# Block attention on the two 64x64 corners of each block, and the values' product in two half arrays

## The chip, the cores and the metric

The kernel runs on one core of one Trainium2 chip. The metric is the device time of one execution in microseconds. The kernel before takes 242.04 us in the median of 3 runs (241.68 to 242.35). Matrix products run on TensorE (PE; its weight loads are PEld), elementwise work on VectorE (DVE), ScalarE (ACT) and GpSimd (POOL), and DMAs are issued by SyncE (SP).

## What is computed

The input x has 2048 tokens of 448 features. The result is h2 = h + B(h) with h = x + A(x).

A is attention with 16 heads of 28 features on the normalised x. Token s sees only the eight keys s, s-2, ..., s-14:

```
qkv = layernorm(x) @ wqkv            # 448 -> 3 * 448
idx = pos[:, None] - 2 * arange(8)   # positions below 0 are masked
logits = q . k[idx] * 28 ** -0.5
o = softmax(logits) @ v[idx]
A = o @ wo
```

B is a gated MLP that mixes tokens:

```
z = gelu(layernorm(h) @ w_in)        # 448 -> 2 * 896, halves z1 and z2
g = w_sp @ layernorm(z2) + b_sp      # w_sp is 2048 x 2048, over tokens
B = (z1 * g) @ w_out                 # 896 -> 448
```

## The kernel before

**Who sets the order.** The kernel builds a list of jobs, each with an engine, the operations, what they read and write, and a place in PSUM. `ORDER` (line 26) is a written-out permutation of the jobs, and each engine and the DMA queue of SP work off their jobs in that order, waiting on semaphores where a job needs another's result. `BANK` gives each PSUM ticket its bank, `ON` says which engine does a copy that several could do. PSUM has eight banks of 512 columns; nearly all products take two banks at once, so that about four of them are open at a time.

**Products in halves.** Most products contract over 448 features, in chunks of 64. `product` (line 480) splits each into a part A of eight matmuls and a part B of six, alternately in the upper and the lower 64 rows of the array, into two banks. In part B each bank is served by the other half than in part A, so part B waits until part A has ended, and `apart` demands that another PE job stands between.

**Stages.** x is loaded in six pieces and normalised per 128 tokens (xn). The first four pieces of 128 tokens are transposed by PE, the other twelve by DMA transposes, into xhT. Then the queries and keys (`qk`, five token ranges `QT` by four groups of heads) and V are computed. Attention works on 18 blocks of 112, 114 or (the first) 128 queries; each block sees 128 keys, the queries' own and the 14 or 16 before (`GEOM`, `pad`). After every 256 tokens `project` computes y = o @ wo, h, its norm and the DMA transpose hT. The first and second half of w_in follow (z2, z1; line 825 on), then the product with w_sp (`g`, line 908), the gate, and w_out (line 932). w_in and w_sp are loaded by the same SP queue that issues the transposes.

**The block.** For each block:

- `lg` (line 763), two jobs for heads in two pairs of row strips: one matmul per head, keys stationary (28 rows, 128 columns), the block's queries streamed (112, 114 or 128), each at its own row strip of 32. Heads come in groups of four; head hh of a group lies at rows 32*hh. Each job has two PSUM banks.
- `ex` (line 772), two jobs: ScalarE takes the exponential of all 128 x 8*nq logits into E, bf16.
- `mk` (line 778): VectorE multiplies E by a 0/1 mask `maskb`, the band of the eight keys, the same for all heads.
- `o` (line 787): per head one matmul over all 128 keys, E stationary (128 x 128), V with a column of ones streamed (29 columns), all in one bank.
- `rc`, `om` (lines 795, 798): the reciprocal of the sums, and o times it, into otm; `od` copies the last 64 columns once more, and `oT` is a DMA transpose.

E has four slots, so a block's exp waits for the values' product four blocks before. A small fill (`pads`, line 581) zeroes the columns behind a slot's last head. The matrices of the mask are made by nine steps on GpSimd (line 585 on).

The three kinds of products use the array in different shapes: 64-row halves (`product`), 32-row strips over all columns (`lg`), and the whole array (`o`, `g`, w_out).

## Time and profile before

| what | value |
|---|---|
| runs | 242.04 us median, 241.68 to 242.35 |
| the profiled execution | 240.89 us, of which its span, first to last instruction, 239.2 |
| granted TensorE clock | 1.000 |
| ScalarE: exp, 36 | 32.0 us busy |
| VectorE: mask, 18 | 19.6 us busy |
| PE: logits, 288 matmuls | 92 ns a weight load |
| DMA | 23.26 MB, 66310 packets |

Columns of a group of instructions: line, engine, operation, output<-inputs, shapes, count, then busy time in us and the mean length of one in ns, then the idle time of the engine just before them and what ended it. Matmuls are pipelined: a record of one lasts longer than the time until the next one starts, so what a run of matmuls costs is read from start to start. A timeline row has start, length, engine, line and count, and in brackets the idle time before it.

### The profile page before, as it was taken

The page shows a single profiled execution, that of the slowest core. Times are in us where ns is not written, and L with a number is a line of the kernel's source. Part 1 is how long each engine was busy: PE and PEld are TensorE (multiplying, and loading weights), DVE is VectorE, ACT ScalarE, POOL GpSimd, SP SyncE. Part 2 cuts the span into 40 slices and gives each one's busy share as a digit, 9 for nine tenths or more (in the row PEclk, how much of TensorE's full clock was granted, in tenths as well). Part 3 has the DMA queues.
Part 4 walks back from the last instruction along what each step waited for, and adds up shares of the span by engine and source line. Part 5 has one row for each costly group of instructions (what it writes and reads, how often), then busy time and mean ns, then how long its engine had stood idle before and what let it go on. Part 6 is the DMA issues. An engine that isn't in the chain of part 4 may idle for free.

```text
span 239.2 us, 4969 instructions
## 1 busy us (share of the span) xinstructions
PE 231.4 (97%) x2099; PEld 114.3 (48%) x2110; DVE 152.3 (64%) x323; ACT 92.0 (38%) x113; POOL 35.2 (15%) x73
## 2 busy tenths in 40 slices
PE   7989999799999999999999999999999999999995
PEld 2564464354555644444444444444444444444453
DVE  5799799979989987959877124410751222613674
ACT  3787988768789656687820000000000000000000
POOL 5154220440302030313124000000000000000000
DMA  6943538526668967979999970000000010000032
GB/s 202 340 119 69 137 70 142 89 60 124 148 106 165 171 108 157 154 149 165 168 192 166 186 189 0 3 0 0 0 0 3 31 47 0 0 3 0 26 108 97
DMA packets 66310, 23.26 MB, mean 97 GB/s; under 512 B 58608, under 2 KB 66160, under 8 KB 66288
## 3 DMA queue, kind: packets, MB, share of 16 engines
q1 hardware_dynamic: 66288, 22.95, 47.1%
q8 instruction: 16, 0.26, 0.4%
q14 instruction: 6, 0.05, 0.1%
HBM read 6.83 MB, written 1.84 MB: 36 GB/s over the span
## 4 chain that ended last, share of the span: by engine, by line
PE 81%; DVE 9%; DMA 4%; ACT 2%; SPq 2%; issue 1%; POOL 0%
PE psum L908 40%; PE psum L495 27%; PE psum L932 9%; DMA x_tm<-in_A_x_dram 3%; PE psum L763 2%; PE psum L787 2%; DVE st L607 2%; DVE E L778 2%; DMA xhT<-xn 2%; ACT E L772 1%; DVE z2p L505 1%; DVE otm L798 1%; SPq L520 1%; SPq L519 1%; DVE xn L618 1%
## 5 line engine op out<-in xcount | busy, mean ns | idle before, releaser
L908 PE MATMUL psum<-wsp_hi,z2p 128*128 128x512 bf16 x218 | 50.6, 379 | 0.3
L917 DVE TENSOR_TENSOR ub<-psum,bb 128x512 bf16<-128x512 f32 x28 | 19.2, 689 | 44.4 <-PE psum L908 43.9
L772 ACT ACTIVATE E<-psum 128x896 bf16<-128x896 f32 (+2 forms) x36 | 32.0, 934 | 9.0 <-PE psum L763 9.0
L908 PEld LDWEIGHTS psum<-wsp_hi,z2p 128*128 128x128 bf16 x224 | 21.9, 98 | 26.1
L495 PE MATMUL psum<-xhT,wqk 64*128 64x512 bf16 (+1 forms) x280 | 27.1, 334 | 2.0 <-DMA xhT<-xn 1.6
L908 PE MATMUL psum<-wsp_lb,z2p 128*128 128x512 bf16 x108 | 26.1, 379 | 0.2
L908 PE MATMUL psum<-wsp_la,z2p 128*128 128x512 bf16 x111 | 25.9, 379 | 0.2 <-issue 0.2
L495 PE MATMUL psum<-w_in,hnT 64*128 64x448 bf16 x224 | 24.8, 349 | 0.1
L495 PE MATMUL psum<-hnT,w_in 64*128 64x512 bf16 x196 | 24.1, 376 | 0.0
L939 DVE TENSOR_TENSOR srg<-psum,x_tm 128x448 bf16<-128x448 f32 (+1 forms) x17 | 9.7, 592 | 20.8 <-PE psum L932 20.7
L932 PE MATMUL psum<-w_out,z1p 128*128 128x448 bf16 (+1 forms) x119 | 22.3, 341 | 0.0
L843 DVE BATCH_NORM_STATS2 st<-z2p 128x6 f32<-128x448 bf16 x32 | 18.9, 609 | 3.7 <-ACT z2p L836 3.4
L778 DVE TENSOR_TENSOR E<-E,maskb 128x1792 bf16<-128x1792 bf16 (+2 forms) x18 | 19.6, 1095 | 1.7 <-ACT E L772 1.6
L607 DVE BATCH_NORM_STATS2 st<-x_tm 128x6 f32<-128x448 bf16 x32 | 19.4, 612 | 1.6 <-DMA x_tm<-in_A_x_dram 1.4
L602 POOL TENSOR_TENSOR rs<-rs,negh 128x2 f32<-128x2 f32 (+2 forms) x22 | 18.9, 857 | 1.8
L495 PEld LDWEIGHTS psum<-xhT,wqk 64*128 64x128 bf16 x280 | 12.8, 94 | 12.3 <-ACT E L772 2.4
L908 PEld LDWEIGHTS psum<-wsp_la,z2p 128*128 128x128 bf16 x112 | 10.9, 98 | 13.4 <-DVE z2p L852 0.4
L908 PEld LDWEIGHTS psum<-wsp_lb,z2p 128*128 128x128 bf16 x112 | 11.0, 98 | 13.2
L932 PEld LDWEIGHTS psum<-w_out,z1p 128*128 128x128 bf16 x119 | 11.6, 98 | 10.2 <-DVE z1p L920 0.3
L880 ACT ACTIVATE z1p<-psum 128x1024 bf16<-128x1024 f32 x14 | 14.2, 1023 | 5.2 <-PE psum L495 5.1
L495 PEld LDWEIGHTS psum<-w_in,hnT 64*128 64x128 bf16 x224 | 10.6, 94 | 11.0 <-DVE z2p L505 0.6
L601 POOL TENSOR_SCALAR rs<-mv 128x2 f32<-128x2 f32 (+2 forms) x22 | 6.3, 288 | 62.1 <-DVE mv L609 41.3
(54 smaller groups left out, 226.2 us busy)
## 6 DMA issues: line engine op xcount, KB each, us to landing
w_in<-in_B_w_in_dram SPq DMA_DIRECT2D x8, 224.0 KB, 3.0
out_dram<-srg SPq DMA_DIRECT2D x16, 112.0 KB, 1.7
x_tm<-in_A_x_dram SPq DMA_DIRECT2D x3, 448.0 KB, 6.1
wraw<-in_A_wqkv_dram SPq DMA_DIRECT2D x2, 448.0 KB, 4.1
w_out<-in_B_w_out_dram SPq DMA_DIRECT2D x1, 784.0 KB, 6.4
bb<-in_B_b_sp_dram SPq DMA_DIRECT2D x1, 512.0 KB, 5.8
wv<-in_A_wqkv_dram SPq DMA_DIRECT2D x2, 224.0 KB, 6.3
wo<-in_A_wo_dram SPq DMA_DIRECT2D x1, 336.0 KB, 7.7
```

What stands on the lines that cost most here:

```text
L495: ins = e.matmul(out(k), w(k, p0, c), x(k, p0, c), start=(k, p0, c) in first, stop=(k, p0, c) in last, tile_position=(p0, 0))
L601: [(lambda e: e.tensor_single_scalar(A, mv[:, m:m + n, 1], EPS, ALU.add), r_mv[k][m:m + n], [rr]), (lambda e: e.tensor_tensor(R, A, negh[: ...
L602: (lambda e: e.tensor_tensor(R, A, negh[:, 0:1].to_broadcast([128, n]), ALU.pow), [rr, r_negh], r_rs[k][m:m + n])],
L607: [(lambda e: e.bn_stats(st[:, m, :], src), [rsrc], [r_st[k][m]])], dve_t(D))
L772: return e.activation(o, i, AF.Exp, scale=SCALE)
L778: return e.tensor_tensor(a, a, maskb[:, 0:1, pad:pad + nq].to_broadcast([NK, NHEAD, nq]), ALU.mult)
L843: [(lambda e, m=m, k=k: e.bn_stats(st3[:, m, k, :], z2p[:, m, D * k:D * (k + 1)]), [r_z2[m]], [r_st[2][m]])], dve_t(D))
L880: return e.activation(o, i, AF.Gelu_apprx_tanh)
L908: ins = e.matmul(psv(tk), z2p[:, s, 128 * fc:128 * fc + 128], w[:, 512 * (tc % 2):512 * (tc % 2) + 512], start=(s == 0), stop=(s == NB - 1))
L917: [(lambda e, tc=tc, s=s, tk=tk: e.tensor_tensor(ub[:, s, :], psv(tk), bb[:, 512 * tc:512 * tc + 512], ALU.add), [r_bb], [r_ub[s]])], dve_ ...
L932: ins = e.matmul(psv(tk, 0, c1 - c0), z1p[:, fc, 128 * m:128 * m + 128], w_out[:, fc, c0:c1], start=(fc == 0), stop=(fc == FC7 - 1))
L939: [(lambda e, m=m, s=s, tk=tk, c0=c0, c1=c1: e.tensor_tensor(srg[:, s, c0:c1], psv(tk, 0, c1 - c0), x_tm[:, m, c0:c1], ALU.add), [r_x[m]], ...
```

## The change

**Logits.** A block's 128 keys are cut at 64. Keys 0 to 63 are seen only by the block's first 64 queries (78 in block 0) and keys 64 to 127 only by its last 64. So each head has two matmuls of 64 keys by 64 queries, at column tiles 0 and 64 of its row strip: the upper one writes PSUM partitions 0 to 63, the lower one 64 to 127. From block 1 on all 16 heads share one ticket of two banks, 64 columns per head; the second job `lg_1` writes the same banks from other strips and must wait for the end of `lg_0`.

**Exp and mask.** From block 1 on one exp of 1024 columns per block, and a mask of 16 x 64 columns, at a stride of 128 in E. The other 64 columns of each head stay zero; they are filled once at the start per slot (`pads0` to `pads3`, two on VectorE and two on GpSimd), and `padsx` clears 14 columns after block 0. The mask is made in 14 steps instead of nine, with three variants.

**Values' product.** Per head two matmuls with 64 keys each, one per 64-row half of the array, with the same 128 x 128 reading of E (zeros beside the corner); heads 0 to 7 and 8 to 15 have a bank each, and, as in `product`, part B serves each bank from the other half. The ticket has two banks, and `rc` and `om` read both.

**Order.** `ORDER`, `BANK` and `ON` are new for all jobs. On PE logits now stand mostly in groups of four halves (`lg4_0 lg5_0 lg4_1 lg5_1`), once of eight, in eight stretches; parts A and B of the values' product stand between parts of other products. On VectorE the fills `pads2` and `pads0` come before the first statistics and between the first two normalisations; normalisations 2 and 3 come before the statistics of rows 4 to 7 are all done. On SP some w_in loads and the transposes of w_sp for slices 6, 1, 4 and 7 come earlier, among the transposes of xn and o.

```
-        pool("pads", -58, [(lambda e: e.memset(E[:, :, NHEAD * 112:NHEAD * 114 + 14], 0.0), ...
+        def ez(i):
+            return E[:, i, 0:NHEAD * 128].rearrange("p (h c) -> p h c", c=128)[:, :, 0:64]
+        for i in range(NE):
+            move_z("pads%d" % i, [(lambda e, i=i: e.memset(ez(i), 0.0), [], [r_Ez[i]]),
...
+            wd, u0 = (78, 64) if b == 0 else (64, nq - 64)
+            tk2 = Ticket(2)
             for j in range(2):
-                tk = Ticket(2)
+                tk = Ticket(2) if b == 0 else tk2
...
-                            c = (tk.b + i) * 512 + 128 * g
-                            ins = e.matmul(psum[:, c:c + nq], qkT[p:p + DH, 2 * g + 1, k0:k0 + NK],
-                                           qkT[p:p + DH, 2 * g, t0:t0 + nq], start=True, stop=True,
-                                           tile_position=(p, 0))
+                            c = (tk.b + i) * 512 + (128 * g if b == 0 else 64 * (4 * j + g))
+                            for r in range(2):
+                                ins = e.matmul(psum[64 * r:64 * r + 64, c:c + wd], qkT[p:p + DH, 2 * g + 1, k0 + 64 * r:k0 + 64 * r + 64],
+                                               qkT[p:p + DH, 2 * g, t0 + u0 * r:t0 + u0 * r + wd], start=True, stop=True,
+                                               tile_position=(p, 64 * r))
...
+                if b and not j:
+                    continue
...
+            if b:
+                pl.apart.append((lgs[(b, 0)], lgs[(b, 1)]))
...
-                        ins = e.matmul(psum[:, tk.b * 512 + 32 * h:tk.b * 512 + 32 * h + DH + 1],
-                                       E[:, slot, ei * nq:ei * nq + 128], V1[:, vs, h, 0:DH + 1],
-                                       start=True, stop=True)
+                        for r in range(2):
+                            k = part ^ r
+                            ei = 8 * (hh % 2) + 4 * (hh // 2) + 2 * k + gg
+                            c = (tk.b + k) * 512 + 32 * (4 * gg + hh)
+                            a = 64 + 128 * ei - u0 * r
+                            ins = e.matmul(psum[:, c:c + DH + 1], E[64 * r:64 * r + 64, slot, a:a + 128],
+                                           V1[64 * r:64 * r + 64, vs, 4 * (2 * k + gg) + hh, 0:DH + 1], start=part + gg + hh == 0, stop=part + gg + hh == 5,
+                                           tile_position=(64 * r, 0))
```

## The prediction

> **What bounds the kernel now.** The page first: busy time by engine, two rows of the forty slices, and the shares of the chain that ended last.

> ```profile
> span 239.2 us, 4969 instructions
> ...
> PE 231.4 (97%) x2099; PEld 114.3 (48%) x2110; DVE 152.3 (64%) x323; ACT 92.0 (38%) x113; POOL 35.2 (15%) x73
> ...
> PE   7989999799999999999999999999999999999995
> ...
> DVE  5799799979989987959877124410751222613674
> ...
> PE 81%; DVE 9%; DMA 4%; ACT 2%; SPq 2%; issue 1%; POOL 0%
> ```

> TensorE is busy nearly throughout, and the chain that ended last lies on it for 81%. A busy PE may still run under its rate, so the next views are the waits, and the stretch from the start of the query and key product of tokens 512 on to the first product with w_sp (start and end, length, then busy time of PE, PEld, DVE, ACT, POOL).

> ```profile
> POOL rs L601 <- DVE mv L609: 41.3, 12, 7.8
> ...
> PE psum L495 <- DMA xhT<-xn: 1.6, 1, 1.6
> ...
> PE psum L647 <- DVE xn L618: 0.8, 1, 0.8
> ```
> ```profile
> 21.20:118.70 97.50, 95.61 (x1323) 48.62 (x1321) 85.77 (x178) 75.17 (x87) 21.94 (x38) 1.00 0.72 130
> ```

> In the waits (us in total, times, longest) PE waits visibly for two things, 2.4 us together, at full granted clock (1.00). In the window, which ends at that first product, VectorE is busy 85.8 and ScalarE 75.2 of 97.5 us, and PE 95.6. So work taken from ScalarE and VectorE is worth only the waits that it ends. What else the change can bring must come from PE's own time for logits and values' product. From the first product with w_sp on the change computes nothing differently; only the order of products differs, PE has no gap there now, and I take the rest as a constant.

> The price of these products is start to start, since records of matmuls overlap. In the chain of waits, and in the timeline of PE below it, they read:

> ```profile
> 23.42 4.42 PE psum L495 x40
> 27.84 0.90 PE psum L787 x32
> 28.74 0.30 PE psum L763 x8
> ...
> 30.42 0.49 PE psum L787 x16
> ...
> 32.43 0.33 PE psum L763 x16
> ...
> 118.70 10.74 PE psum L908 x49
> ```
> ```profile
> 51.23 0.92 PE L495 MATMUL psum<-wv,xhT 64*128 64x448 bf16 x8
> 51.98 0.81 PE L495 MATMUL psum<-xhT,wqk 64*128 64x512 bf16 x6
> ...
> 58.42 0.92 PE L495 MATMUL psum<-wv,xhT 64*128 64x448 bf16 x8
> 59.27 0.96 PE L787 MATMUL psum<-V,E 128*128 128x29 bf16 x32
> ...
> 78.21 1.76 PE L787 MATMUL psum<-V,E 128*128 128x29 bf16 x64
> 79.91 0.93 PE L495 MATMUL psum<-w_in,hnT 64*128 64x448 bf16 x8
> ```

> Sixteen value matmuls take 0.49, 64 take 79.91 - 78.21 = 1.70: (1.70 - 0.49)/48 = 25 ns each, and 0.09, say 0.10, once per run. Eight half-array matmuls take 51.98 - 51.23 = 0.75 before another half-array product, but 59.27 - 58.42 = 0.85 before the values' product: entering another shape of the array costs 0.10, leaving it 0.10 again (that second one is inside the 0.49 and 0.33). Eight logits matmuls on two row strips, four per strip, take 0.30: 0.10 for leaving, and 50 ns from one to the next on a strip. Sixteen on four strips take 0.33: the strips run side by side. Forty matmuls of the query and key product take 4.42, 0.22 a pair.

> **Part by part: the values' product.** Before: 288 x 25 ns + 11 runs x 0.10 = 8.3 us.

> ```profile
> L787 PE MATMUL psum<-V,E 128*128 128x29 bf16 x288 | 9.0, 176 | 0.0
> ...
> L763 PEld LDWEIGHTS psum<-qkT 28*128 28x128 bf16 x288 | 5.0, 92 | 5.5 <-issue 1.6 <-ACT E L772 1.1 <-DVE xn L618 0.7
> ...
> L763 PE MATMUL psum<-qkT 28*128 28x112 bf16 x144 | 4.7, 210 | 0.0
> ```
> ```profile
> 13.40 0.37 PE L763 MATMUL psum<-qkT 28*128 28x112 bf16 x8
> ...
> 71.72 0.40 PE L763 MATMUL psum<-qkT 28*128 28x114 bf16 x16
> ```

> After: 576 matmuls on 64 rows, alternately in the two halves, in 36 jobs of 16. If the halves run side by side, a job is 8 x 25 ns = 0.20 and all are 7.2 us; if not, it is 16 x 25 ns = 0.40 and all are 14.4. Less than 25 ns on one piece of the array no row shows. I take 7.2, as sixteen logits matmuls in 0.33 already beat 16 x 25 = 0.40. The array's shape is now that of the products around it, so no switch: -1.1 us. The part-B job waits for part A's end; one other job lies between always, so I cost that at nothing; uncovered it would be about 0.2 (a matmul's 176 ns) each.

> Entries into other shapes: before, the nineteen logits runs (the first and the last are above) and eleven value runs form 23 stretches, 2.3 us; after, eight logits stretches, 0.8. That is -1.5.

> **Logits.** Before: 17 runs x 0.33 + 2 x 0.30 = 6.2 us. After: 36 halves of 16 matmuls, four on each of four tiles (two row strips by two column halves), 64 columns streamed instead of 112, 64 columns of weights instead of 128. No row shows a column tile. Lower bound: 25 ns per interval, the shortest of any row, 0.10 a half. Upper bound: the load is not hidden at all, 92 ns from its row and 50 x 64/112 = 28 ns of streaming, 120 ns, 0.48 a half. I take 50 ns, 0.20 a half, the nearest row (the run of eight: same strips, loads hidden, though twice as many columns loaded and streamed). In a group of four halves, first halves a0 and b0 of two blocks, then a1 and b1 into the same banks: a1 starts when a0's last result is in, 0.15 + 0.21 = 0.36; b1 ends at 0.20 + 0.36 + 0.20 = 0.76; leaving makes 0.86 for two blocks, 7.7 us for eighteen. By the same steps 25 ns gives 0.59 and 5.3 us, 120 ns gives 1.75 and 15.7. So +1.5, between -0.9 and +9.5.

> [...]

> **Exp, mask, fills.**

> ```profile
> L772 ACT ACTIVATE E<-psum 128x896 bf16<-128x896 f32 x18 | 16.1, 923 | 5.3 <-PE psum L763 5.3
> ...
> L778 DVE TENSOR_TENSOR E<-E,maskb 128x1792 bf16<-128x1792 bf16 x9 | 9.8, 1086 | 1.7 <-ACT E L772 1.6
> ...
> L772 ACT ACTIVATE E<-psum 128x1024 bf16<-128x1024 f32 x2 | 2.0, 1024 | 0.6 <-PE psum L763 0.5
> ...
> L778 DVE TENSOR_TENSOR E<-E,maskb 128x2048 bf16<-128x2048 bf16 x1 | 1.2, 1215 | 0.0
> ```
> ```profile
> 1.51 0.48 DVE L582 MEMSET otm<- 128x512 uint32 x1
> ...
> 5.55 0.41 DVE L618 TENSOR_SCALAR xn<-x_tm,mv,rs 128x512 bf16<-128x512 bf16 x1 [0.47 <-POOL rs L602]
> ```

> Seventeen blocks have one exp of 1024 instead of two of about 900: 2 x 0.92 - 1.02 = 0.82 each, 14 us off ScalarE. The mask falls from 1792 to 1024 columns at (1215 - 1086)/256 = 0.5 ns: 1.09 to 0.70, 6.6 us off VectorE; if the strided form lost its rate the saving would be nothing. The fills cost VectorE twice 0.5 (the 1024 values go in pairs, like the 0.48 above) to 1.0 at the start, and one of about 0.3 after block 0's product, with block 0's scaling (om0) queued behind it. One start fill stands between the first two normalisations, with 0.47 us of idle time as cover; it may push the second by 0.1 to 0.5, and I cost that at nothing because ScalarE's weight repack stands before the copy that needs it. Two fills and five more mask steps go to GpSimd, which idles for 41 us in all before statistics (its wait for DVE mv). Copies that change engine go about as many each way; I take them as nothing. All this is off the path; its worth is the waits.

> **Waits.**

> ```profile
> 7.65 3.32 PE L495 MATMUL psum<-xhT,wqk 64*128 64x256 bf16 x56 [0.34 <-ACT xhT L505]
> ...
> 12.74 0.72 PE L647 MATMUL psum<-ident,xn 128*128 128x128 bf16 x8 [0.80 <-DVE xn L618]
> ...
> 47.41 1.04 PE L495 MATMUL psum<-xhT,wqk 64*128 64x512 bf16 x8 [1.62 <-DMA xhT<-xn]
> ```
> ```profile
> 14.39 12.73 SPq L519 DMA_TRANSPOSE xhT<-xn  x8
> ...
> 36.05 1.20 SPq L519 DMA_TRANSPOSE xhT<-xn  x1
> ...
> 40.56 4.97 SPq L519 DMA_TRANSPOSE xhT<-xn  x3
> ```

> The 0.80 falls because normalisations 2 and 3 no longer stand behind the statistics of rows 4 to 7 on VectorE. Half is given back: two w_in loads go ahead of the first transposes, and row 4's normalisation comes some 0.6 after the old 14.39, at about 1.3 us a transpose, so the product for tokens 512 on, which starts at 21.2 now, starts near 21.4; meanwhile PE does later blocks' work. Net -0.5 (0 to -0.8). The 1.62 falls because the last four normalisations stand around mask 5 on VectorE. From 21.4 PE does 28 pairs for tokens 512 on (6.1), seven more (1.5), blocks 0 to 2's values (1.2) and the logits of 4 and 5 (1.0): 31; exp and mask make 33, the four with what stands between 37. On SP two w_in loads, wlo1, oT3 and oT4 stand among these transposes; seven or eight issues of 1.3 or less start the last by about 43, and like the others it lands 2 to 3 us on, at 46. It is needed after the whole of the two products for tokens 512 and 1024 on (12.2), V for three pairs of blocks (4.0 at 0.19 a pair), two output projections (2.7), values of blocks 0 to 6 (2.8) and logits of 4 to 11 (3.8): 47, or 48 with small waits. That is -1.6; if the cover of 1 to 2 us is gone, it stays. New: pairs of blocks take their PSUM banks together, four blocks all eight, so PE meets an exp or a V copy still running; about four places x 0.2, +0.8 (0 to 2).

> **Sum.** -1.1 - 1.5 + 1.5 - 0.5 - 1.6 + 0.8 = -2.4 us. The profiled execution took 240.89, its span 239.2 and 1.7 around it; its forecast is 238.5. The median of the runs is 242.04, 1.15 above that execution, so the forecast on its scale is 239.6.

> **Rivals.** (1) Cheaper logits: tiles at 25 ns. -2.4 - 2.4 = -4.8, 237.2. For it: fewer columns loaded and streamed than in the row I took. (2) No change: the products gain 1.1, but transposes or PSUM banks make PE wait as before, or the product gain is used up. 0 to -0.5, about 242. For it: VectorE's many 9s up to slice 20, and SP's queue. (3) Slower: loads of column tiles show. At 120 ns the logits take 15.7 instead of 7.7: +8.0 - 2.4 = +5.6, 247.6. It decides from about 77 ns per interval, where two blocks cost 1.29 instead of 0.86 and the 2.4 is gone. Against it: loads hide on row strips now, as 50 ns with a 92 ns load shows. [...] (4) It does not do what it says: the array's halves take turns in the values' product, +7.2 - 2.4 = +4.8, 246.8. Against it: 0.33 for sixteen.

> **Numbers.** Forecast 0.47, its own range 238.1 to 241.1; (1) 0.15, (2) 0.16, (3) 0.16, (4) 0.06. About 0.3% (0.7 us) is what a measurement can tell from no change. Faster: nearly all of the forecast and (1), 0.61; same 0.15; slower 0.24, from (3), (4) and a bad (2). The range goes from 236.8, (1) with fewer new waits, to 244.5, which takes in (2) and (3) to about 90 ns, and leaves out the rest of (3) and (4).

> **What would show it.** Right: value matmuls at 8 x 25 ns per 16 with no gap to their neighbours; a group of four logits halves near 0.86; no PE wait on xhT near 47; the product with w_sp starting near 116.3 instead of 118.7; about 120.5 after it, as now. Wrong: that start after 118; intervals above 77 ns on a column tile; PE rows that wait on ACT E or on V copies for over 2 us in all; a later first product than 7.65.

## The result and the profile after

The changed kernel takes 246.64 us in the median of four executions (244.38 to 248.66), beside 242.19 for the kernel before. The ratio of the two is taken over their faster executions alone, here 245.12 and 244.38, since 248.17 and 248.66 lie over 1.5% above the fastest: 1.011 times as long (95% interval 1.007 to 1.015). Measured again it was 1.017 (1.009 to 1.025) and 1.011 (1.006 to 1.016). It is slower; the forecast was 1% faster. The profiled execution took 245.12, 4.23 more than the one before.

The page of the changed kernel: the first line counts all instructions, PEclk is the granted clock of TensorE in tenths by slices of a fortieth, q8 is the DMA queue that the page calls `instruction` (packets, MB, share); its packets have 16,384 bytes each.

```profile
span 243.4 us, 6131 instructions
...
PEclk9999997999999999999999999999999999999999
...
q8 instruction: 21, 0.34, 0.6%
```

And the same queue in the kernel before:

```profile
q8 instruction: 16, 0.26, 0.4%
```

There are 1162 instructions more, five more packets, and one slice with a lower clock. I take the packets for TensorE's instructions: its records (products, weight loads, its sequencer's) are 4268 before and 5433 after, 267 and 259 to a packet. The waits of TensorE in the changed kernel (who waited <- for whom: us in all, times, longest):

```profile
PE psum L496 <- DMA OT<-otm: 1.8, 1, 1.8
...
PE psum L665 <- DVE xn L636: 0.9, 2, 0.7
PE psum L496 <- DMA xhT<-xn: 0.7, 1, 0.7
PE psum L496 <- DVE OT L506: 0.6, 1, 0.6
PE psum L785 <- DVE qkT L506: 0.6, 1, 0.6
PE psum L820 <- DVE E L807: 0.6, 1, 0.6
PE psum L973 <- DVE z1p L961: 0.4, 1, 0.4
PE psum L820 <- issue: 0.2, 1, 0.2
```

The wait of 1.62 us for xhT near 47 us is gone, as forecast. In its place stand one of 1.8 us for a transposed attention output and a row of waits of about half a microsecond. (A name in front of a line number is what is written: `qkT` the queries and keys, E the exponentials, OT the transposed output, xhT the transposed input.) The chain of the same execution (start, length, what):

```profile
33.80 4.36 DMA OT<-otm
38.30 2.50 PE psum L496 x14
...
122.17 51.91 PE psum L949 x240
```

The transpose of block 2's output (oT2) is issued at 33.80 and lands at 38.16. The w_sp product starts at 122.17; it was 118.70 before, and 116.3 by forecast. What follows the long wait shows in a table by stretches (columns after the length: busy time and count for PE, PEld, DVE, ACT, POOL; then the granted clock):

```profile
37.50:38.30 0.80, 0.01 (x1) 0.04 (x2) 0.00 (x0) 0.80 (x2) 0.00 (x0) 1.00 0.33 33
38.30:40.00 1.70, 1.70 (x12) 0.88 (x14) 0.00 (x0) 0.20 (x1) 0.00 (x0) 0.64 0.70 190
40.00:41.50 1.50, 1.50 (x24) 0.77 (x22) 0.00 (x0) 0.65 (x1) 0.00 (x0) 0.50 0.76 128
41.50:43.00 1.50, 1.50 (x27) 0.91 (x24) 0.82 (x1) 0.37 (x1) 0.00 (x0) 0.77 0.90 165
```

From 38.79 on, by the trace's clock records, the clock is at one half for 3.41 us, which costs TensorE 1.7 us.

The products themselves, in the timeline of TensorE (start, length, line, count):

```profile
31.86 0.87 PE L785 MATMUL psum<-qkT 28*64 28x64 bf16 x64
32.66 1.04 PE L496 MATMUL psum<-xhT,wqk 64*128 64x512 bf16 x8
```

Four logits halves take 0.80 from start to start (0.86 by forecast). And at the start, VectorE's timeline:

```profile
4.68 0.41 DVE L636 TENSOR_SCALAR xn<-x_tm,mv,rs 128x512 bf16<-128x512 bf16 x1 [0.29 <-POOL rs L620]
5.15 0.48 DVE L592 MEMSET E<- 128x512 uint32 x1
5.70 0.09 DVE L593 MEMSET E<- 128x32 uint32 x1
5.71 0.87 DVE L636 TENSOR_SCALAR xn<-x_tm,mv,rs 128x512 bf16<-128x512 bf16 x1
```

The fill stands between the first two normalisations, and the second takes 0.87 where it took 0.41: GpSimd fills another slot of E at that time. The first product of TensorE starts at 8.04 instead of 7.65.

Where the 4.2 us are, from start to start in both traces:

| part | forecast | measured |
|---|---|---|
| first product | 0 | +0.4 |
| products: values, shapes, logits | -1.1 | -0.2 by the rows after and the prediction's count of before, -0.9 by the rows of both (the shapes' -1.5 taken as forecast); -0.5 by what is left over |
| waits over 0.15 us ahead of the w_sp product | -1.3 | +2.0 (2.4 in two places, now 4.4 in six) |
| halved clock | none | +1.7 |
| behind the start of the w_sp product | 0 | +0.6 |

(The chain gives +0.7 for the last, 120.5 to 121.2; the trace of before lacks the record of the first w_sp product, 0.2 us, so that its row of 118.70 is late by that. The wait for z1p lengthens one interval by 0.59.)

### The profile page after: what moved, and what is told of

Its sections match the earlier page's. It is cut to its first block, busy times and chain, and to the rows that moved or that the text cites. A ratio compares the mean times of both kernels' runs of the same rounds, so it can differ in the third digit from the quotient of the medians.

```text
span 243.4 us, 6131 instructions
## 1 busy us (share of the span) xinstructions
PE 233.3 (96%) x2688; PEld 120.4 (49%) x2688; DVE 146.5 (60%) x327; ACT 81.8 (34%) x99; POOL 33.4 (14%) x79
## 3 DMA queue, kind: packets, MB, share of 16 engines
HBM read 6.83 MB, written 1.84 MB: 36 GB/s over the span
## 4 chain that ended last, share of the span: by engine, by line
PE 78%; DVE 9%; DMA 7%; ACT 2%; issue 1%; POOL 1%; SPq 1%; POOLq 0%
PE psum L949 38%; PE psum L496 28%; PE psum L973 8%; DVE st L625 2%; DMA x_tm<-in_A_x_dram 2%; PE psum L820 2%; DMA OT<-otm 2%; DMA OTs<-otm 2%; DMA xhT<-xn 2%; DVE E L807 1%; DVE xn L636 1%; DVE ub L958 1%; ACT qkT L506 1%; DVE mv L627 1%; POOL rs L620 1%
## 5 line engine op out<-in xcount | busy, mean ns | idle before, releaser
L496 PE MATMUL psum<-xhT,wqk 64*128 64x512 bf16 (+1 forms) x280 | 29.1, 339 | 0.7 <-DMA xhT<-xn 0.7
L506 ACT ACTIVATE qkT<-psum 128x1024 bf16<-128x1024 f32 (+1 forms) x18 | 15.3, 859 | 16.1 <-PE psum L496 16.1
L798 ACT ACTIVATE E<-psum 128x1024 bf16<-128x1024 f32 x17 | 16.6, 1028 | 4.0 <-PE psum L785 3.8
L620 POOL TENSOR_TENSOR rs<-rs,negh 128x2 f32<-128x2 f32 (+2 forms) x22 | 17.1, 776 | 1.8
L496 PE MATMUL psum<-wo,OT 64*128 64x448 bf16 x112 | 14.2, 367 | 2.5 <-DMA OT<-otm 1.8
L820 PEld LDWEIGHTS psum<-V,E 64*128 64x128 bf16 x576 | 12.3, 93 | 8.6 <-DVE E L807 1.9
L496 PEld LDWEIGHTS psum<-w_in,hnT 64*128 64x128 bf16 x224 | 11.3, 94 | 9.6 <-ACT OT L506 0.2
```

Source lines behind the costliest of these rows:

```text
L496: ins = e.matmul(out(k), w(k, p0, c), x(k, p0, c), start=(k, p0, c) in first, stop=(k, p0, c) in last, tile_position=(p0, 0))
L506: j = pl.job(name, eng, key, [(lambda e: e.activation(o(), i(), AF.Copy) if eng == "act" else e.tensor_copy(o(), i()), list(reads), list(w ...
L620: (lambda e: e.tensor_tensor(R, A, negh[:, 0:1].to_broadcast([128, n]), ALU.pow), [rr, r_negh], r_rs[k][m:m + n])],
L798: return e.activation(o[:, :, :, 0:64], psum[:, tk.b * 512:tk.b * 512 + 1024].rearrange("p (i h q) -> p i h q", i=2, q=64), AF.Exp, scale= ...
L820: ins = e.matmul(psum[:, c:c + DH + 1], E[64 * r:64 * r + 64, slot, a:a + 128], V1[64 * r:64 * r + 64, vs, 4 * (2 * k + gg) + hh, 0:DH + 1 ...
```

## The experiments

The theory after the traces: the products came out near the forecast, and the time was lost in the new order, through a late transpose and the clock after it, VectorE beside GpSimd's fills, and the tail. The first rival: the new products cost more than their rows show. The second: what makes transposes late, instruction fetches, is there in any order.

### 1. The changed kernel again, and four edits of its order

**e0_control**, no edit.

> The changed kernel again, unaltered, on the chip and in the job of the three runs beside it, as their yardstick. Theory (the time was lost in waits, not in the products): 244 to 246 us; TensorE waits about 1.8 us near 36.4 us of the span for the transposed output oT2, its granted clock then stands at 0.5 for about 3.4 us, the w_sp product starts near 122.2 us and about 121.2 us follow it. Rival (the 245 us of the first profile was one unlucky execution): within 0.3% of the kernel before, and the wait near 36.4 us not there or short.

245.85 us median of four, 1.017 (1.009 to 1.025). The profiled execution took 243.65, and there the wait for oT2 and the halved clock are both absent. So neither is a constant of this kernel. Its oT2 stands at the same place in the queue and is issued at 33.26, and it lands 2.46 us later instead of 4.36; the queue's order alone doesn't make the long wait. Still this execution is 2.7 us longer than the one before: first product +0.4, waits +2.2 (eight of 0.2 to 0.8), tail +0.6, products -0.5. Of 18 executions of the changed program 11 have a clock below 1, seven of them by two such spells (0.985 or 0.986); of 115 executions of the kernel before 62 have one, all of them by a single spell (0.992 or 0.993). The halved clock is in both kernels; two spells in one execution are in the changed one alone.

**e1_sp_order**: jobs on SyncE's queue.

```
-xTdma8 w_in1_1 wlo6 oT1 oT0 oT2 xTdma14 w_in1_0 oT3 wlo1 xTdma13
+xTdma8 oT1 w_in1_1 oT0 oT2 xTdma14 oT3 xTdma13 w_in0_0 ... xTdma15 w_in1_0 ... hT8 wlo6 hT10 wlo1
```

> The changed kernel with four weight loads later in SyncE's written order (second half of w_in1 behind the transpose oT1, the w_lo load 6 behind hT8, w_lo load 1 behind hT10, first half of w_in1 behind the last xT transpose), so that the transposes oT0 and oT2 are issued some 2 to 4 us earlier; nothing that TensorE computes is altered. Theory (the new order put these loads ahead of oT2 on SyncE's queue, TensorE waits 1.8 us for it and its clock is then halved for 3.4 us, which costs another 1.7 us): wait and clock dip near 37 us go, the w_sp product starts 2.5 to 3.6 us earlier, near 119, and the time falls to 241.5 to 243 us. Rival 1 (the column-tiled logits and the halved values' product cost TensorE itself more): the wait goes but the time stays within 0.7 us, since the products and not the wait are what came on. Rival 2 (the transposes are late because instruction fetches fall on their DMA engines, wherever they stand in the order): another transpose is late by 1 to 2 us instead, and the time falls by less than 1 us.

243.52 us, 1.005 (1.002 to 1.009): faster than the changed kernel, by about half of what was expected. In its chain:

```profile
120.95 51.91 PE psum L940 x240
```

The w_sp product starts 1.2 us earlier than at first, not 2.5 to 3.6, and 0.3 later than in e0_control, whose transpose had landed in time without help. In this profile the long wait is gone, and the short ones stand as before. Four of its ten executions still have a lower clock, three of them by two spells.

**e2_fills**: VectorE and GpSimd (fill 0 to 3 are `pads0` to `pads3`).

```
-DVE: n0_0 pads0 n0_1 wp0_1_0        POOL: rs0_1 pads1 ... mask13 pads3
+DVE: n0_0 n0_1 pads0 wp0_1_0 ... st0_10 pads1      POOL: mask12 pads3 mask13
```

> The changed kernel with the start's zero fills of E moved: fill 0 on VectorE behind the second normalisation instead of between the first and the second, fill 1 from GpSimd to VectorE behind the statistics of block 10, fill 3 on GpSimd behind the last mask operation. Theory (VectorE is held up by the fill itself, 0.57 us, and runs at half speed while GpSimd fills): the second normalisation takes 0.4 us again instead of 0.86, the normalisation of block 8 0.4 to 0.6 instead of 1.17, TensorE's first product starts near 7.65 instead of 8.04 us, block 1's mask is done earlier, and the time falls by 0.4 to 1 us, as far as nothing behind it (the wait for oT2 near 36.4 us) takes it back; the waits later in the span keep their places. Rival (the start's delay is absorbed by the wait near 36 us): the first product comes earlier by 0.4 us, and the time stays within 0.2 us.

245.66 us, 1.013 (1.005 to 1.021): no gain. VectorE's timeline shows that the mechanism is there:

```profile
5.64 0.41 DVE L627 TENSOR_SCALAR xn<-x_tm,mv,rs 128x512 bf16<-128x512 bf16 x1 [0.47 <-POOL rs L611]
6.11 0.48 DVE L583 MEMSET E<- 128x512 uint32 x1
```

The second normalisation is back at 0.41, that of block 8 went from 1.17 to 0.40, and the wait for block 1's mask is gone. But the fill now stands ahead of the weight copies, the first product starts at 8.54, and in the profiled execution a transpose later on (oT4) was late by 3.2 us, with a halved clock behind it. The theory was right on the operations and wrong on the time.

**e3_hold_clock**: a job ahead of the output projection of block 0.

```
+pl.job("hold", "pe", 1e6, [(lambda e: [e.matmul(psv(tkh, 0, 128), ident[:], ident[:], start=True, stop=True)
+                                       for _ in range(27)][-1], [r_ident], [])], 1.5, acq=tkh)
```

> The changed kernel with 27 products of the identity matrix (128 columns, about 1.5 us at full clock, into a free PSUM bank that nobody reads) on TensorE in the idle time just ahead of the output projection of block 0, where it waits 1.8 us for oT2. They compute nothing that the output uses. Theory (TensorE's idle time of 1.8 us is what makes the granted clock stand at 0.5 for the next 3.4 us): the wait itself stays, since oT2 lands no earlier, but the clock stays near 1.0 from 38 to 42 us and the time falls by about 1.7 us, to near 243.4. Rival (the dip's cause is something else, the load of the column-tiled products just ahead, or a throttle that comes at times of its own): the clock falls to 0.5 all the same, and the time rises by up to 1.5 us or stays.

The stretches around it in TensorE's clock:

```profile
36.00:37.50 1.50, 1.50 (x78) 1.43 (x77) 1.50 (x4) 0.68 (x2) 0.63 (x1) 1.00 0.42 79
37.50:40.00 2.50, 2.50 (x43) 1.67 (x42) 0.27 (x1) 1.42 (x2) 0.00 (x0) 1.00 0.55 134
40.00:42.00 2.00, 2.00 (x52) 1.20 (x48) 1.14 (x2) 1.02 (x1) 0.00 (x0) 1.00 0.60 122
```

oT2 lands at 38.10 here too, and the clock stays at 1.00: at this place the idle time halves it, and without the idle time the products ahead of it don't. Three of four executions had a clock of 0.999 or more. That part holds. The time doesn't follow: 247.19 us, 1.020 (1.014 to 1.025), against an expected 243.4. TensorE stops elsewhere, for 1.2 us near 64 in the middle of a run of logits that wait for nothing, and 0.5 near 49; it also waits 1.6 for a transpose hT near 109 and 1.1 near 23.6. The stops were the first sign of what section 6 settles.

**e4_both**, e1_sp_order and e2_fills together.

> The later weight loads of e1_sp_order and the moved fills of e2_fills together, everything else as in the changed kernel. Theory (two separate losses of the new order, and the waits for the mask of block 1 and for the second normalisation go with the fills): the fills give 0.4 to 0.9 us beside the 1.1 to 2.2 us of the later loads, so 242 to 243 us, level with the kernel before or up to 0.4% slower; no wait of over 1.5 us ahead of the w_sp product and no halved clock in most executions. Rival (a wait that is taken away is given back at the next late transfer): the time stays within 0.2% of e1_sp_order.

245.60 us, 1.014 (1.007 to 1.021), worse than e1_sp_order alone. No wait exceeds 0.9 us, yet every execution has a halved clock; in the profile three waits of 0.25 to 0.85 us stand within five microseconds ahead of it. Neither the theory nor the rival expected a loss.

### 2. More instructions, and the old order

**e5_nops** and **e6_phase** were to add empty instructions, to the kernel before and to the changed one.

```
+for _ in range(3):
+    e.nop()
 ins = e.matmul(out(k), w(k, p0, c), x(k, p0, c), ...
...
-block.tensor(lambda eng: sch.emit("pe", eng))
+block.tensor(lambda eng: ([eng.nop() for _ in range(128)], sch.emit("pe", eng)))
```

> The kernel before with 1113 empty instructions (NoOp) on TensorE, three ahead of each product of the stages qk, v, y and z2; nothing is computed otherwise. They bring TensorE's instructions to 5,320, near the changed kernel's 5,376. Theory (instructions are fetched in blocks of 16 KB over the same DMA engines; each fetch lengthens a DMA-transpose issue by 0.7 to 1.2 us and makes transposes land late): the instruction queue's packets rise from 16 to 20 or 21, more of SyncE's transpose issues ahead of 90 us take 1.8 us or longer, TensorE waits longer for transposes, and the time rises by 0.5 to 2.5 us, with the product intervals unchanged. Rival 1 (fetches are hidden): the packets rise and the time stays within 0.3%. Rival 2 (empty instructions cost TensorE itself): the intervals of the products with the added instructions grow, evenly.

> The changed kernel with 128 empty instructions (8 KB, half of a fetched block) ahead of TensorE's first work, where TensorE waits for data anyway; all else as it was. Theory (a late transpose is one on which an instruction fetch falls): every fetch comes half a block earlier, some 2 to 2.5 us in the stretch from 25 to 85 us; the issue of transpose oT0, which took 1.86 to 2.64 us in all five traces of the changed kernel's orders, takes 1.3 us, another transpose some 2 us ahead of it in the order takes about 2, and which waits show changes with it. The time changes by up to 2 us in either direction. Rival (oT0 is slow for what stands ahead of it in the queue): the same issues stay long, the waits keep their places.

The programs hold no empty instructions: 16 and 21 packets, as without them. So the two runs are repeats: 0.9998 (0.995 to 1.004) for the kernel before, 1.011 (1.006 to 1.016) for the changed one. They say nothing on fetches.

**e7_old_order**: `ORDER` and `ON` of before on the changed jobs, PSUM banks handed out first-free.

> The changed kernel's products, exp, mask and fills (fills where e2_fills has them) in the order of the kernel before: its order of jobs, its engines for the copies, and PSUM banks handed out first-free; the second half of a block's logits and of its values' product stands one TensorE job behind the first half. Theory (the products by themselves are worth about nothing and the new order lost the time): 240.5 to 242.5 us, within 0.3% of the kernel before or faster, and the w_sp product starts near 118.5 us. Rival (the new products, with two PSUM banks for the logits of 16 heads and two for the values' product, make TensorE wait for banks whatever the order): TensorE waits for ACT's exp and DVE's normalisation by more than 3 us in all, and the time is 244 us or more.

267.08 us, 1.101 (1.093 to 1.110). TensorE waits 13 us in 22 places ahead of the w_sp product, and its clock is halved for 20.5 us in three spells of 6.83. The longest row of waits:

```profile
PE psum L487 <- DVE otm L831: 4.0, 6, 1.1
```

These are PSUM banks that block results hold until VectorE has scaled them. The run fits the rival, but my bank choice is part of it, so it doesn't separate products from order. One thing it shows: with the old order of the tail, from the first w_sp product to the last product it is 118.06 us, against 118.67 in the changed order.

### 3. Position in the program, the tail, one corner

**e9_phase**: five of the first warming products replaced.

```
+pl.job("phase", "pe", 1e6, [(lambda e: [e.matmul(psv(tkp, 0, 8), warm[:, 0:128], warm[:, 0:8], start=True, stop=True)
+                                        for _ in range(64)][-1], [r_warm], [])], 1.5, acq=tkp)
```

> The changed kernel, with five of the warming products at TensorE's start replaced by 64 narrow ones (8 columns), which brings 118 more instructions, nearly half of a fetched block of 256, ahead of all that follows; TensorE waits for data there anyway. Theory (TensorE runs out of instructions: in every trace of the changed order it stops 0.2 to 1.2 us in the middle of a run of products that wait for nothing, behind the eight logits halves of blocks 12 to 15, and goes on some 2.5 us after an instruction packet set out): every packet comes about half a block earlier in the program, so the stop near 64 to 66 us moves to another place in that dense stretch or goes, the issue of transpose oT0, 1.9 to 2.6 us in most traces so far, falls back to about 1.3 and another transpose ahead of it takes about 2. The time changes by up to 1.5 us in either direction. Rival (the stops hang on the data, not on the fetches): the stop stays in the same value product, and the same issues stay long.

247.36 us, 1.019 (1.013 to 1.026). The stop in mid-product is gone from 64 us and from all the stages (0.24 us stand ahead of a warming product at 4.0), but the issue of oT0 takes 1.75 us, not the 1.3 that was expected. But the start is lost:

```profile
7.09 2.34 PE L979 MATMUL psum<-warm 128*128 128x512 bf16 x5
9.36 0.34 PE L487 MATMUL psum<-xhT,wqk 64*128 64x256 bf16 x2
```

Five warming products take 2.3 us where they took 1.2 in e0_control, 427 ns from start to start instead of 216, so TensorE ran at half the rate. The first product starts 1.3 us later, which spoils the time as evidence. That the stop went speaks for the theory.

**e10_tail**: TensorE and VectorE.

```
-PE: g3_3_3 wo11_0 g2_3_1 wo9_0 wo4_0 ... g5_3_3 wo8_0 wo12_0
+PE: g3_3_3 wo11_0 g2_3_1 wo9_0 ... g5_3_3 wo4_0 wo8_0 wo12_0
```

> The changed kernel with the output product of token block 4 moved behind the last group of the w_sp product, so that two output products instead of one stand between that group and the product which needs its last result. Theory (the tail of the new order is 0.6 us longer than the old one for that single wait of TensorE for VectorE's z1p): the wait goes, and from the first w_sp product to the last product of TensorE it is 118.1 us instead of 118.7; the time falls by 0.5 to 0.6 us against the changed kernel, whatever the earlier waits do. Rival (VectorE's last steps are the bound, not their place): the wait moves to the next output product and the tail stays at 118.5 us or more.

245.17 us, 1.010 (1.005 to 1.014). The wait for z1p is gone, and the tail is 118.06 us, as in the old order (117.84 in its trace, which lacks the record of the first w_sp product, 0.22). The 0.6 us are there; the long wait and the clock ahead of it come as before (1.8 us in its profile).

**e11_tuned**: e1_sp_order, e10_tail, the loads w_in2_0 and w_in3_0 behind hT0, fill 0 behind the weight copies, fill 1 on VectorE and fill 3 early, qe1_0 (a copy of queries and keys out of PSUM) ahead of the statistics of block 11.

> The changed kernel with the later weight loads of e1_sp_order, two more of them behind the transpose hT0 (so that oT8, whose landing frees the buffer that block 11's result waits for, is issued 1.3 us sooner), the tail of e10_tail, the zero fills of E moved out of the first normalisations' way and behind the weights' copies, and the copy qe1_0 one statistics step earlier on VectorE. Theory (the loss is waits of the new order, each of which can be moved out of the way): first TensorE product near 7.8 us instead of 8.05, no wait for qe1_0 and for block 1's mask near 18 to 22 us, none for om11 near 60, tail 118.1; in all 2 to 3 us below the changed kernel, 241.5 to 243 us, within 0.4% of the kernel before on either side. Rival (what is won ahead is waited for at the next late transpose or instruction packet): no more than 1.5 us below the changed kernel, above 243.5.

243.71 us, 1.007 (1.003 to 1.010): 2 us below the changed kernel and 0.7 above the theory's 243, with two new waits of 0.6 us at the start where the fills went and one of 1.2 for a mask near 23.

**e12_onetile**:

```
-for r in range(2):
-    ins = e.matmul(psum[64 * r:64 * r + 64, c:c + wd], qkT[p:p + DH, 2 * g + 1, k0 + 64 * r:k0 + 64 * r + 64], ...
+ins = e.matmul(psum[:, c:c + wd], qkT[p:p + DH, 2 * g + 1, k0:k0 + NK],
+               qkT[p:p + DH, 2 * g, t0:t0 + wd], start=True, stop=True, tile_position=(p, 0))
```

> The changed kernel with one logits product per head over all 128 keys and the block's first 64 or 78 queries, in place of two of 64 keys: the second corner is left out (its place holds logits of other queries), and 288 products and as many weight loads go; exp, mask, values' product and order stay. Theory (column-tiled logits cost TensorE some 1.5 us themselves, and their instructions come faster than they are fetched): instruction packets fall from 21 to 18 or 19, the stop in the middle of a values' product near 64 us goes, the logits' busy time falls by 1.5 to 3.5 us, idle time ahead of the w_sp product by 0.5 to 1; 240 to 243 us. Rival 1 (loads of the tiles were hidden and the instructions too): the time stays within 0.5% of the changed kernel, since the waits of the order take up what the logits give. Rival 2 (the stop is a wait for data): it stays.

244.43 us, 1.007 (1.002 to 1.011). In its page and timeline:

```profile
q8 instruction: 19, 0.31, 0.6%
```
```profile
31.90 0.76 PE L775 MATMUL psum<-qkT 28*128 28x64 bf16 x32
32.59 1.04 PE L487 MATMUL psum<-xhT,wqk 64*128 64x512 bf16 x8
```

Half the products take 0.69 from start to start instead of 0.80. The column tiles cost 0.1 us a group, 1.0 us of the logits' busy time in all (8.1 in e0_control, 7.0 here), less than the 1.5 to 3.5 expected; the time is above the 240 to 243 expected. Packets fall to 19 and the stop goes, as the theory had it; the idle time falls by 0.4 only, since a wait of 1.0 us for a PSUM bank takes its place. With the rows of the values' product in the changed kernel (8.1 us against 8.3) the first rival of this chapter, dear products, falls.

### 4. The same work in more instructions

**e13_split**, on the kernel before.

```
+cut = 2 if name[0] in "qvy" and n > 256 else 1
...
+    for s in range(cut):
...
+            ins = e.matmul(o[:, s * h:s * h + h], w(k, p0, c), v[:, s * h:s * h + h], ...
```

> The kernel before, in its own order, with each wide product of the stages qk, v and y (512 or 448 columns) issued as two of half the width: the same sums, 406 more products and as many more weight loads, 812 instructions or some 3 packets of 256, all ahead of 75 us. Theory (instruction packets lengthen transpose issues and make them land late): packets ahead of 90 us rise from 10 to 13, SyncE's transpose issues of over 1.5 us from 5 or 6 to 8 or more, nearly all of them over a packet; TensorE's idle time ahead of the w_sp product rises by 0.5 to 2 us with its busy time within 0.5 us, and the time by 0.3 to 1%. Rival 1 (fetches are hidden, and the new order alone makes late transposes matter): as many more packets and long issues, but idle time and time the same within 0.3%. Rival 2 (half-width products show their weight loads): the busy time rises by more than 1 us.

244.69 us, 1.012 (1.007 to 1.016). In its stretches (PE's busy time is the second number):

```profile
8.26:121.04 112.78, 109.35 (x1928) 76.85 (x1930) 98.23 (x213) 85.94 (x104) 26.07 (x51) 1.00 0.75 132
121.04:240.30 119.26, 117.50 (x556) 55.14 (x565) 49.41 (x100) 2.63 (x3) 4.21 (x8) 1.00 0.23 51
```

Busy time rises by 1.1 us (rival 2: half-width products show their loads), idle time ahead of the w_sp product by 0.7, the first product starts 0.6 later, and one wait of 1.2 us near the end is a matter of result buffers. Packets ahead of 90 us are 12, long transpose issues 6, hardly more than in the kernel before. So this run doesn't show that packets alone make a kernel slower; whether late transposes cost time in an order not packed so densely stays open.

### 5. Taking the waits away

**e14_best**: e1_sp_order, e10_tail, w_in2_0 and w_in3_0 behind hT0. **e15_best2**: also fill 3 behind mask step 12. **e16_best3**: also

```
-DVE: n0_2 n0_3 st0_7         POOL: od13     PE: y10A o16A y10B z2_6A o16B
+DVE: st0_7 n0_2 n0_3  od13                  PE: o16A y10A o16B y10B z2_6A
```

> The changed kernel with the later weight loads of e1_sp_order, two more behind the transpose hT0, and the tail of e10_tail; the fills stay as changed. Theory (three separate losses of the new order): 1.1 to 2.2 us from the loads, 0.6 from the tail, up to 0.4 from oT8: 242 to 243 us, within 0.3% of the kernel before, and most executions without a halved clock. Rival (with 14 instruction packets ahead of 90 us some transpose is late in any order): still 0.4% or more slower than the kernel before, with a halved clock in every second execution.

> As e14_best, with fill 3 of E earlier on GpSimd (behind the mask step 12), so that the normalisation of block 8 doesn't run beside it. Theory (VectorE is held up while GpSimd fills, and block 1's mask with it): the normalisation of block 8 takes 0.4 instead of 1.17 us, the wait of 0.56 us for block 1's mask near 21.7 us goes, and the time is 0.2 to 0.5 us below e14_best. Rival (the next transpose, xT of block 7, lands no earlier and takes the gain back): no difference beyond 0.2 us.

> As e15_best2, with the statistics of block 7 ahead of the normalisation of block 2 on VectorE (in 0.65 us that stood idle there, so that blocks 4 to 7 are normalised and their transposes issued 0.6 us sooner), od13 on VectorE instead of GpSimd (0.18 instead of 0.63 us, so that transpose oT13 is issued sooner), and block 16's values' product ahead of the output projection that waits for oT13. Theory (the gain of the products, some 0.5 us, is behind the waits): the waits near 22 and 77.5 us shrink from 0.8 and 0.7 us to 0.3 or less each, and the time falls by 0.5 to 1.2 us against e15_best2, to 241.3 to 242, 0 to 0.4% below the kernel before. Rival (each wait taken away comes back at the next late transpose or instruction packet): within 0.2% of e15_best2.

e14_best: 242.70 us, 1.003 (1.000 to 1.007); six of its twelve executions have a halved clock, as its rival had it. e15_best2: 242.47, 1.002 (0.999 to 1.005); the normalisation of block 8 and the mask came as expected, the wait for xT of block 7 took part of it back. e16_best3: 241.85 us beside 242.43 for the kernel before, 0.9993 (0.996 to 1.003). With the changed order's waits taken away one by one the changed products are level with the kernel before, and no more than that. Its w_sp product starts at 119.15.

### 6. Where a fetched block ends

The trace of e16_best3 has one wait that no job explains. TensorE's timeline:

```profile
61.56 0.30 PE L811 MATMUL psum<-V,E 64*128 64x29 bf16 x11
62.79 0.24 PE L811 MATMUL psum<-V,E 64*128 64x29 bf16 x5 [0.94 <-issue]
```

A values' job of sixteen products stops behind the eleventh for 0.9 us, with no semaphore between. "issue" is time in which the profile shows nothing to wait for.

**e17_phase2** changes only how the warming products are cut.

```
-[e.matmul(psv(tkw), warm[:, 0:128], warm[:], start=True, stop=True) for _ in range(1)]
+[e.matmul(psv(tkw, 0, 128), warm[:, 0:128], warm[:, 0:128], start=True, stop=True) for _ in range(4)]
```

**e18_best4** is e17_phase2 with fill 0 ahead of the other early fill and fill 1 on VectorE.

> As e16_best3, with each of the 15 warming products of 512 columns at the start issued as four of 128 columns: the same columns streamed, 90 more TensorE instructions, so that every fetched block of 256 ends about a third of a block earlier in the program. Theory (the stop in mid-product near 62 us is an empty instruction store, and hangs on where a block's end falls in the dense stretch of blocks 12 to 15): the stop moves to another place or shrinks, by 0.3 to 0.9 us, and so does the time, at most; the packets come some 1 to 2 us sooner. The start stays within 0.2 us. Rival (the stop is due to the density of the stretch alone, wherever the blocks end): it stays at 0.5 to 1.0 us.

> As e17_phase2, with fill 0 of E in place of another early fill of VectorE (which goes behind the normalisation of block 10) and fill 1 on VectorE behind the statistics of block 10, where it waits for GpSimd anyway. Theory (GpSimd's fill slows the second normalisation from 0.41 to 0.86 us and fill 0 stands ahead of it): that normalisation ends 1 us sooner, near 5.6 us of the span, the wait of 0.65 us near 6.1 us shrinks to 0.2, and 0.2 to 0.5 us of that reaches the time: 240.8 to 241.6 us, 0.3 to 0.6% below the kernel before. Rival (the first product waits for the weights, and the next transposes for their blocks, so that nothing of it comes through): within 0.2% of e17_phase2.

e17_phase2: 245.54 us, 1.013 (1.008 to 1.017), against 0.9993 without the 90 instructions. Its waits and its timeline:

```profile
PE psum L776 <- issue: 3.6, 3, 2.0
```
```profile
62.01 1.33 PE L776 MATMUL psum<-qkT 28*64 28x64 bf16 x74
65.36 0.58 PE L776 MATMUL psum<-qkT 28*64 28x64 bf16 x26 [2.02 <-issue]
```

Against my expectation the stop didn't shrink. It moved into the logits group and grew to 2.0 us, and two more appeared, at 20.8 (0.6) and 46.2 (1.0). The same work in the same order is 1.3% slower, where blocks of instructions end elsewhere. Not all of it is the stops themselves, 2.7 us more than in e16_best3: that profile also has a wait of 1.1 us for a result buffer and a clock halved for 10.2 us in all instead of 3.4. e18_best4 has the same three stops, in an execution at full clock:

```profile
PE psum L776 <- issue: 3.4, 3, 2.0
```

It takes 246.04 us, 1.015 (1.010 to 1.019); the second normalisation took 0.41 and nothing of it came through.

I counted all of TensorE's records by start (products, weight loads and the few of its sequencer). All 20 stops ahead of an instruction that waits for no semaphore, apart from the one in e9_phase's warming, lie in 14 traces at the same places: records 705, 1985 and 2753, which is 193 + 256n for n = 2, 7, 10, whatever job stands there. (The other rows of "issue", 1.87 us in e18_best4 and 0.56 in e13_split among them, stand at the first product of a job that does wait for a semaphore.) Each of the 20 ends 2.3 to 3.0 us after the n-th packet of q8 set out. That packet set out with 39 to 198 records left to the stop. In the kernel before, TensorE reaches record 256n + 193 at the earliest 5.6 us after the n-th packet; in the changed one 2.5 us after the tenth, in e17_phase2 2.3 to 3.0 us after three of them. A dense group of eight logits halves is 256 records in 1.7 us. I read the stops as TensorE running out of instructions: what it needs from 256n + 193 on would come with the n-th packet, 256 records to 16,384 bytes. That is an inference, from the positions, the times of the packets and the shift in e17_phase2; no record shows the fetch of a single instruction. In the kernel before no stop shows at these places, in the changed one there are stops.

The clock has one more side, which e3_hold_clock doesn't reach. Its spells last 3.41 us or twice that, and those of one trace begin whole multiples of 3.41 us apart. Two stretches of 3.41 us, each with the one that follows it, from e10_tail and from e18_best4 (columns as in the tables by stretches above):

```profile
63.35:66.76 3.41, 3.08 (x157) 2.02 (x149) 2.58 (x8) 3.41 (x5) 0.71 (x1) 1.00 0.39 80
66.76:70.17 3.41, 3.32 (x59) 1.56 (x63) 2.10 (x5) 1.29 (x2) 0.00 (x0) 0.50 0.77 97
```
```profile
64.19:67.60 3.41, 1.80 (x56) 1.20 (x57) 1.57 (x4) 2.11 (x3) 0.00 (x0) 1.00 0.99 90
67.60:71.01 3.41, 2.98 (x102) 1.72 (x100) 3.02 (x6) 1.72 (x3) 0.00 (x0) 1.00 0.94 113
```

In e10_tail TensorE idles for 0.33 us in the first stretch, and the clock is halved in the next; in e18_best4 it idles for 1.61, and the clock stays. The stretch of e10_tail holds the eight logits halves of blocks 12 to 15, and the second spell of e6_phase (67.59) and of e11_tuned (66.78) begins behind the same group. So idle time alone doesn't set the clock, and the dense group of small products may itself cost a spell of 1.7 us; no run here takes it apart.

## Why the prediction was wrong

It said 239.6, faster, in 236.8 to 244.5; the median was 246.64. By its own steps:

- **Values' product**, -1.1 from 0.20 a job. The 36 jobs take 0.224 on average, 8.1 us in place of 8.3: -0.2. The mechanism was right (the halves work side by side, nearly every job within 0.20 to 0.24), the size was not: a job takes some 24 ns more than the eight intervals of 25 ns that I counted.
- **Other shapes**, -1.5. No gap stands around the new jobs, and nothing contradicts it; no run measured it by itself.
- **Logits**, +1.5. By my count of before, 1.45 measured: 0.80 a group instead of 0.86. But that count was low. Of the nineteen runs of before, six take 0.37 to 0.57 from start to start and not 0.33, 6.9 us in all and not 6.2, so that the logits cost only some 0.8 more than before. Four half tiles take 32 ns together, beside loads recorded at 105 ns each, and the second half of a block starts 0.1 us behind the first. Rival 3, loads that show, falls; e12_onetile puts the price of the tiles at 1.0 us. (Two figures of that rival don't come out: by the steps of the other cases a group at 120 ns comes to 1.63, not 1.75, and 0.43 more a group at 77 ns would be 3.9 us over nine groups, not 2.4. Nothing here hangs on them.)
- **Start and fills**, costed at nothing. +0.4. I covered the fill by the weight repack and overlooked that GpSimd's fill runs beside the second normalisation and doubles it: 0.87 beside the fill of 0.95 us, 0.41 without it in e2_fills. VectorE didn't stand for the whole of the fill, which ran on for 0.72 us, or the normalisation would have taken 1.13.
- **Waits**, "-0.5 - 1.6 + 0.8". This is the step that failed. The two old waits went as I said. For the new ones I took "about four places x 0.2" of PSUM banks. The waits come to 4.4 us where I had 2.4 of before taken away and 0.8 put in their place, 2.0 longer instead of 1.3 shorter: 1.8 for oT2 in that execution (I had followed the queue behind w_in and wlo for the xn transposes, not for the outputs); 0.6 to 0.7 each for qk, the mask, xhT and oT. At most one of them, that for the copy of queries and keys, can be a wait for a bank. That they hang on operations moved by the new order is shown by e10_tail and e14 to e16: moved again, those for qk, the mask, oT and z1p go, and 0.5 for xhT is left.
- **Clock**, not in the sum: +1.7 us in the profiled execution. Behind the idle time of 1.8 us the clock stands at 0.50 for 3.41 us, and e3_hold_clock shows that the idle time is the cause there. What causes the second spell, near 67 us, stays open.
- **Instructions**, not in the sum. 1162 more, and in dense groups. In the profiled execution the stop is only 0.2 us, 0.8 in e0_control; it was the part that I had no term for at all, and e17_phase2 shows that it can be 3.6.
- **Tail**, costed at nothing: +0.6, one output product too few ahead of the wait for z1p.

The tests that I had named gave the right answer one by one: group of logits, no wait near 47, no long waits on exp or V copies were right; the w_sp product after 118, 121.2 behind it and a first product at 8.04 were the three that called it wrong. Rival 2 had the mechanism (transposes make PE wait as before) and a size of zero; none of the rivals had it on the slower side.

What stays open: how much of a late transpose is the fetch. Of 170 transpose issues of over 1.5 us between 13 and 90 us, in 20 traces, 165 overlap a packet; of 647 shorter ones 121 do. That is a coincidence in time, tested by no run that changed packets alone. And e4_both's loss is not explained beyond its clock.

## What to carry to other kernels

Count the instructions of a change as well as its cycles: where short products stand in dense groups, TensorE may use 256 instructions faster than they come (here 256 records in 1.7 us, and stops that end 2.3 to 3.0 us after a packet set out), and the loss then depends on where a block happens to end: here ninety instructions more at the start of the program turned 0.9993 into 1.013. When a written order is replaced, every queue is a term of the sum: list what stands ahead of each transpose that the old trace shows on time, and price the wait and the clock after it. A product made cheaper by a microsecond is worth that only if no transfer is waited for behind it.
